# Swapping the first two loads of a decode kernel: a 256 KB load in 2 KB rows ahead of a 4 MB load in 32 KB rows

## The chip, the cores and the metric

The kernel runs on one core of one Trainium2 chip. Times are device microseconds (us) of a whole execution. The profile's "span" runs from the first to the last instruction and is about 1.2 us shorter. Before, three executions took 659.73, 659.74 and 659.96 us. The check of the result counts a difference as faster or slower only at 2%.

Words used below: a *load* is one copy from memory to the core's on-chip buffers; an *issue* is the instruction that starts it; the *queue* is the list of issued loads that the sixteen DMA engines work off; a *packet* is one row of a load as one engine moves it. K0, V0, K1, V1, K2 are the successive 4 MB pieces of the key and value caches. *wq* and *wo* are the weights of the query and output projections. The *prologue* is the compute work before the loop over the pieces. PE multiplies matrices, DVE and ACT work on vectors, POOL makes constants and small copies, and SP does nothing here but issue loads and wait.

## The reference

One decode step, batch 2, one token: attention over a cache of 8192 positions with 32 heads of 128, then a gated feed-forward layer.

```python
q = layernorm(x) @ wq                       # x: 2 x 512, wq: 512 x 4096
p = softmax(q . k_cache * 128 ** -0.5)      # k_cache, v_cache: 2 x 32 x 8192 x 128, bf16
h = x + (p @ v_cache) @ wo                  # wo: 4096 x 512
n = layernorm(h)
out = h + (relu(n @ W_gate) * (n @ W_up)) @ W_down
```

The caches are 2 x 134 MB, and each byte is used once. All weights together are 12.6 MB.

## The kernel before

The caches pass through four slots of 4 MB (32 KB in each of 128 partitions). K pieces use slots 0 and 2, V pieces 1 and 3. All large loads are issued by one engine, SP, whose instructions run in order. wq borrows slot 3 until the query is made; the last 256 rows of wo (`wo_rows`) go to a scratch area, and the remaining 3.8 MB of wo are loaded later.

```python
def load(s, cache, p):
    nc.sync.dma_start(slot[s][:], kv(cache, p)).then_inc(slot_sem[s], 16)

nc.scalar.dma_start(x_row, A_x[:, 0]).then_inc(sem_x, 16)
nc.sync.dma_start(slot[3][:], A_wq.rearrange("(p c) n -> p (c n)", c=DC)).then_inc(sem_wq, 16)   # 128 rows of 32 KB
nc.sync.dma_start(
    wo_rows, A_wo[128 * DR:].rearrange("(p r) n -> p (r n)", r=2)).then_inc(sem_wl, 16)           # 128 rows of 2 KB
load(0, A_k_cache, 0)      # K0
load(1, A_v_cache, 0)      # V0
load(2, A_k_cache, 1)      # K1
# ... constants, layernorm of x, its transpose xlT (done at 5.5 us; its token is t_xlT)
pe.wait((sem_wq, 16), t_xlT, t_zero)
# ... 32 matmuls make the query (t_q is the token of the last)
# ... the query is laid out for DVE and PE (q_all)
sp.wait(t_q)               # wq has been used: slot 3 is free
load(3, A_v_cache, 1)      # V1
nc.sync.dma_start(X[:], A_wo[0:128 * DR] ...)       # the rest of wo, 3.8 MB
# ...
pe.wait((sem_wl, 16))      # wo_rows are used here, after the query layout
# ... two pairs of matmuls put them into wo_last
dve.wait(t_q_b, t_wl, t_const)                      # then the loop starts
# in the loop, for each piece p:
#   DVE multiplies K by the query (k_mult); after it K's slot is free
sp.wait((d2s, p + 1), tokp("kf", p))
load(s, A_k_cache, p + 2)
```

So V1 can be issued only after the projection has read wq out of slot 3, and K2 only after the first product on DVE, which needs the query and both wo and wq. These are the two ways in which the start can hold up the queue.

The softmax here doesn't subtract the row's maximum and nothing guards it: scores larger than these inputs give would overflow.

## Time and profile before

| | before |
|---|---|
| time, median | 659.74 us |
| span | 658.6 us |
| bytes moved, mean rate | 281.17 MB, 427 GB/s |
| busiest compute engine (DVE) | 71% of the span |
| DMA engines busy with the queue of loads | 99.4% |
| first packet of wq starts | 1.83 us |
| first projection matmul (wq landed) | 12.99 us |
| first K product on DVE | 26.79 us |
| K2 issued | 33.43 us |

These are lines of the page of before: the span, the busy time of the engines, the DMA share in forty slices of the span (tenths), the rate in each slice, the totals and the queue of loads.

```profile
span 658.6 us, 7569 instructions
...
PE 326.1 (50%) x3066; PEld 192.1 (29%) x3067; DVE 469.4 (71%) x280; ACT 214.2 (33%) x433; POOL 72.7 (11%) x125
...
DMA  8999999999999999999999999999999999999997
GB/s 366 445 426 437 426 442 418 442 420 444 424 436 438 422 440 420 444 422 438 430 432 438 422 440 420 444 422 438 440 422 436 424 438 424 440 428 436 434 415 307
DMA packets 10645, 281.17 MB, mean 427 GB/s; under 512 B 1190, under 2 KB 1292, under 8 KB 1804
...
q1 hardware_dynamic: 10628, 281.06, 99.4%
```

What to see: the row of nines. No compute engine is near full, but the queue is, from the first slice to the last. Such a kernel's time is the start of the queue, plus its bytes, plus what comes after the last byte.

The next lines are the timeline of before: start in us, duration in us, engine, line, operation, output<-inputs; in brackets the idle time before it and what ended it. "SPq" lines are issues.

```profile
0.81 0.40 SPq L174 DMA_DIRECT2D slot<-in_A_wq_dram  x1
1.27 0.42 SPq L175 DMA_DIRECT2D prod<-in_A_wo_dram  x1
1.73 0.42 SPq L171 DMA_DIRECT2D slot<-in_A_k_cache_dram  x1
...
12.99 3.58 PE L256 MATMUL O<-slot,xlT 128*2 128x512 bf16 x32 [7.64 <-DMA slot<-in_A_wq_dram]
...
16.61 0.33 SPq L171 DMA_DIRECT2D slot<-in_A_v_cache_dram  x1
...
17.46 1.01 PE L268 MATMUL W<-ident,prod 128*128 128x128 bf16 x8 [0.89 <-DVE prod L265]
...
26.79 6.56 DVE L539 TENSOR_TENSOR prod<-slot,q_c 128x12288 bf16<-128x12288 bf16 x1 [5.78 <-ACT wo_last L328]
...
33.43 0.33 SPq L171 DMA_DIRECT2D slot<-in_A_k_cache_dram  x1
```

Compute waits 7.64 us for wq, so wq looks urgent. But the first K product ends at 33.35 us, K2 is issued then, and three loads (K1, whose first packets are under way, V1 and the rest of wo) are still in the queue.

The trace also holds a record of each packet (start, duration, size). Views of the page do not list them, so they are given here as figures. In the steady part a 32 KB packet takes 1.213 us and one engine starts the next 1.2095 us later; 16 x 32768 B / 1.2095 us is 433 GB/s. The sixteen first packets of wq start at 1.83 to 2.64 us and take 1.39 to 2.22 us, so they lose 0.66 us each on average against 1.213 us. This is called the start-up loss below.

### The profile page before, as it was taken

How to read it: one execution, taken by the hardware profiler on the slowest of the kernel's cores; microseconds unless marked ns; L12 is line 12 of the kernel's file. 1: busy time of each engine (PE TensorE's matmuls, PEld its weight loads, DVE VectorE, ACT ScalarE, POOL GpSimd, SP SyncE). 2: the span in 40 equal slices, each digit the busy share in tenths (PEclk: the TensorE clock that was granted, in tenths of full speed). 3: DMA queues.
4: the chain of work that ended last, by engine and by line, in shares of the span. 5: the costliest groups of instructions: out<-in, count | busy, mean ns of one | idle time of the engine just before them, and what ended most of it. 6: DMA issues, size and time to landing. Idle time of an engine off the chain costs nothing.

```text
span 658.6 us, 7569 instructions
## 1 busy us (share of the span) xinstructions
PE 326.1 (50%) x3066; PEld 192.1 (29%) x3067; DVE 469.4 (71%) x280; ACT 214.2 (33%) x433; POOL 72.7 (11%) x125
## 2 busy tenths in 40 slices
PE   2753444435554354644535453554445454454586
PEld 0431322214332132422213232322323222232354
DVE  1585576788767678776768867677876767787991
ACT  1622332243342233334223243323324322433151
POOL 3001002020200202020020201102020010202000
PEclk9999565565576555576655577555566755557567
DMA  8999999999999999999999999999999999999997
GB/s 366 445 426 437 426 442 418 442 420 444 424 436 438 422 440 420 444 422 438 430 432 438 422 440 420 444 422 438 440 422 436 424 438 424 440 428 436 434 415 307
DMA packets 10645, 281.17 MB, mean 427 GB/s; under 512 B 1190, under 2 KB 1292, under 8 KB 1804
## 3 DMA queue, kind: packets, MB, share of 16 engines
q1 hardware_dynamic: 10628, 281.06, 99.4%
q8 instruction: 5, 0.08, 0.0%
q14 instruction: 4, 0.03, 0.0%
q10 hardware_dynamic: 8, 0.00, 0.0%
HBM read 281.05 MB, written 0.00 MB: 427 GB/s over the span
## 4 chain that ended last, share of the span: by engine, by line
DMA 80%; DVE 18%; issue 1%; SPq 0%; DVEq 0%; PE 0%
DMA slot<-in_A_k_cache_dram 76%; DVE prod L539 16%; DMA slot<-in_B_W_down_dram 4%; DVE prod L548 2%; DVE scores L553 0%; SPq L171 0%; SPq L702 0%; SPq L698 0%; DVE kT L815 0%; DVEq L586 0%; PE O L807 0%; DVEq L590 0%; SPq L175 0%; SPq L174 0%; DVE zi L505 0%
## 5 line engine op out<-in xcount | busy, mean ns | idle before, releaser
L539 DVE TENSOR_TENSOR prod<-slot,q_c 128x12288 bf16<-128x12288 bf16 x32 | 209.9, 6558 | 148.1 <-DMA slot<-in_A_k_cache_dram 141.4
L404 PE MATMUL O<-slot,e 128*16 128x512 bf16 x1024 | 117.2, 609 | 219.3 <-ACT e L494 146.3
L548 DVE TENSOR_TENSOR prod<-prod 128x6144 bf16<-128x6144 bf16 (+3 forms) x128 | 212.3, 1658 | 7.8
L565 ACT ACTIVATE kT<-T 128x1024 bf16<-128x1024 bf16 x128 | 126.2, 1022 | 144.6 <-PE T L380 141.7
L380 PE MATMUL T<-ident_f,slot 128*128 128x128 f32 x512 | 112.8, 376 | 29.4 <-DVEq L586 29.4
L404 PEld LDWEIGHTS O<-slot,e 128*16 128x16 bf16 x1024 | 26.1, 112 | 284.6 <-ACT e L494 172.9
L494 ACT ACTIVATE e<-scores 64x96 bf16<-64x96 f32 x64 | 19.5, 304 | 239.8 <-DVEq L600 237.0
L380 PEld LDWEIGHTS T<-ident_f,slot 128*128 128x128 f32 x512 | 81.9, 193 | 44.4 <-DVEq L586 43.6
L536 POOL COPY q_c<-q_all 128x136 bf16<-128x136 bf16 x32 | 56.3, 1760 | 196.4 <-DVEq L590 152.5
L363 PE MATMUL S<-q_c,kT 128*128 128x4 bf16 x1024 | 47.6, 168 | 39.2 <-ACT kT L565 38.5
L363 PEld LDWEIGHTS S<-q_c,kT 128*128 128x128 bf16 x1024 | 39.6, 104 | 66.8 <-ACT kT L565 65.5
L416 PE MATMUL Ob<-sel,os_sb 128*128 128x4 f32 x136 | 31.0, 351 | 24.0 <-ACT os_sb L568 24.0
L416 PEld LDWEIGHTS Ob<-sel,os_sb 128*128 128x128 f32 x136 | 29.5, 319 | 25.9 <-ACT os_sb L568 25.9
L519 POOL MEMSET O_l<- 128x40 bf16 (+1 forms) x13 | 1.8, 136 | 303.9 <-DVEq L597 303.9
L553 DVE TENSOR_REDUCE scores<-prod 128x96 f32<-128x768 bf16 x32 | 30.5, 953 | 2.8
L565 ACT ACT_TABLE_LOAD x15 | 19.2, 1283 | 0.3
L494 ACT ACTIVATE e<-S 64x32 bf16<-64x32 f32 x64 | 13.0, 203 | 15.1 <-PE S L363 14.7
L568 ACT ACTIVATE os_sb<-O 128x512 f32<-128x512 f32 x17 | 10.2, 597 | 11.6 <-PE O L404 11.3
L494 ACT ACTIVATION_READ_ACCUMULATOR e<-S 64x1 f32 x64 | 12.8, 201 | 0.7
L494 ACT ACTIVATION_READ_ACCUMULATOR e<-scores 64x1 f32 x64 | 11.8, 184 | 0.0
L425 PEld LDWEIGHTS Ob<-zs,ones_f 128*128 128x128 f32 x30 | 7.1, 294 | 12.8 <-issue 12.8
L524 POOL COPY rsel<-rows 128x30 bf16<-128x30 bf16 x28 | 5.9, 209 | 33.3 <-DVEq L597 32.5
(104 smaller groups left out, 90.6 us busy)
## 6 DMA issues: line engine op xcount, KB each, us to landing
slot<-in_A_k_cache_dram SPq DMA_DIRECT2D x32, 4096.0 KB, 32.1
slot<-in_A_v_cache_dram SPq DMA_DIRECT2D x31, 4096.0 KB, 30.3
slot<-in_A_wq_dram SPq DMA_DIRECT2D x1, 4096.0 KB, 12.1
X<-in_A_wo_dram SPq DMA_DIRECT2D x1, 3840.0 KB, 46.0
slot<-in_A_v_cache_dram SPq DMA_DIRECT2D x1, 3072.0 KB, 23.1
slot<-in_B_W_up_dram SPq DMA_DIRECT2D x1, 1376.0 KB, 21.7
slot<-in_B_W_gate_dram SPq DMA_DIRECT2D x1, 1376.0 KB, 24.7
slot<-in_A_v_cache_dram SPq DMA_DIRECT2D x1, 1024.0 KB, 25.2
```

Source lines behind the costliest of these rows:

```text
L363: i = nc.tensor.matmul(Sp[p % 2][:, 2 * jj:2 * jj + 4], lhsT=kv_[:, k, r, :], rhs=q_c[p % 2][:, 4 * r:4 * r + 4], start=(r == 0), stop=(r ...
L380: i = nc.tensor.transpose(Tp[g % 2][:, k * 128:(k + 1) * 128], k_t[:, j:j + 2, :].rearrange("p j d -> p (j d)").bitcast(F32), ident_f[:])
L404: i = nc.tensor.matmul(Op[0][c:c + 16, :], lhsT=e_t[q][:, j // VJ, :], rhs=v_t[:, j:j + VJ, :].rearrange("p j d -> p (j d)"), start=(q == ...
L416: i = nc.tensor.matmul(Ob[:, 0:4], lhsT=os_sb[:, jj * Dh:(jj + 1) * Dh], rhs=sel[:, 4 * jj:4 * jj + 4], start=(jj == 0), stop=(jj == VJ - 1))
L425: return nc.tensor.matmul(bank[:, ZC:ZC + 8], lhsT=ones_f[:], rhs=zs[:], start=True, stop=True)
L494: i = nc.scalar.activation(out=e_t[q][h, j0 // VJ:j1 // VJ, 8 * q:8 * q + 8].rearrange("p g (j a) -> p g j a", a=2)[:, :, :, a], in_=src(h ...
L536: nc.gpsimd.tensor_copy(out=q_c[p % 2][:], in_=q_all[:, p]).then_inc(g2d, 1)
L539: return nc.vector.tensor_tensor(out=prod[:, 0:JC, :], in0=tile((2 * p) % 4)[:, 0:JC, :], in1=q_c[p % 2][:, 8:QW].unsqueeze(1).broadcast_t ...
L548: run(nc.vector.tensor_tensor(out=prod[:, 0:JC, 0:w], in0=prod[:, 0:JC, 0:w], in1=prod[:, 0:JC, w:2 * w], op=ALU.add))
L553: return nc.vector.tensor_reduce(out=scores[p % PG][:, 0:JC], in_=prod[:, 0:JC, 0:8], axis=AX.X, op=ALU.add)
L565: to_pe(nc.scalar.activation(out=kT[gg % 2][:], in_=Tp[gg % 2][:].bitcast(BF16), func=ACT.Copy))
L568: to_pe(nc.scalar.activation(out=os_sb[:], in_=Op[0][:], func=ACT.Copy))
```

## The change

The intent is to let the program's first load be a small one in short rows, with the big load in long rows behind it. Two issues swap places; nothing is added, removed or resized.

```diff
                 nc.scalar.dma_start(x_row, A_x[:, 0]).then_inc(sem_x, 16)
-                nc.sync.dma_start(slot[3][:], A_wq.rearrange("(p c) n -> p (c n)", c=DC)).then_inc(sem_wq, 16)
                 nc.sync.dma_start(
                     wo_rows, A_wo[128 * DR:].rearrange("(p r) n -> p (r n)", r=2)).then_inc(sem_wl, 16)
+                nc.sync.dma_start(slot[3][:], A_wq.rearrange("(p c) n -> p (c n)", c=DC)).then_inc(sem_wq, 16)
                 load(0, A_k_cache, 0)
```

## The prediction

> **What bounds the kernel now.** One queue of loads that never runs dry. The page counts 281.17 MB at a mean of 427 GB/s over a span of 658.6 us; the queue holds 99.4% of the DMA engines' time, and the forty slices show nine tenths everywhere but in the first and last. In the trace's packet records a steady 32 KB packet starts 1.2095 us after the one before: 16 x 32768 B / 1.2095 us = 433 GB/s. The Trainium skill ("DMA: Bandwidth & Descriptors", Specifications) states a fabric ceiling of 435 GB/s; the trace agrees to half a per cent. The sixteen engines run free of each other: the spread of 0.36 us between them after their first packet is the same seven packets later. So the end is the slowest engine's start plus a fixed amount of work, plus the FFN tail.
>
> **What the change does.** No byte, row or instruction is added; two issues at the head of the queue swap. Before (timeline, packet records):
> - wq is issued at 0.81, wo's rows at 1.27, K0 at 1.73 us; an issue takes 0.40 to 0.42 us.
> - Each engine gets 8 wq packets of 32 KB. The first starts at 1.83 to 2.64 us and takes 1.39 to 2.22 us instead of 1.213: the start-up loss.
> - Each engine's 8 wo packets of 2 KB follow, 0.080 us apart: 0.64 us.
> - The first projection matmul starts at 12.98 us, when wq has landed.
>
> After, wo goes first and wq's packets come 0.64 us later. wq is issued 0.46 us after wo, so its descriptors should be there before wo's work and the start-up loss are over: no bubble, at most 0.1 to 0.2 us in some engine.
>
> **What of it is on the critical path.**
> - wq lands 0.5 to 0.7 us later; the projection, the first K product (26.79 us) and the issue of K2 (33.43 us) slide with it. That is free: when K2 is issued, K1, V1 and the 3.8 MB of wo are still ahead of it, over 25 us of transfer.
> - wo landing earlier is worth nothing: its matmul at 24.3 us waits for the queries.
> - What remains is the start-up. If the loss on the first packets is a matter of time (cold memory, descriptors still being written), nothing changes. If it grows with the packet's length, or comes from sixteen engines starting on rows 32 KB apart, rows of 2 KB save part of some 0.6 us. If the issue cannot feed 2 KB packets, up to 0.2 us is lost.
>
> **Prediction.** 659.5 us, 8 in 10 between 658.8 and 660.2; a change of about -0.2 us. Faster by over 2%: 0.01; within 2%: 0.98; slower by over 2%: 0.01.
>
> **What would show it right or wrong.** Right: the first projection matmul at 13.4 to 13.8 us; K0's packets starting at 12.9 to 13.2 us as before, or up to 0.6 us sooner; the loop's K issues 38.85 us apart per two pairs as before; DMA at nine tenths in all middle slices. The start-up step is wrong if K0's first packets move by more than 0.7 us either way. "No bubble" is wrong if engines stand idle between the last wo and the first wq packet.
>
> **What would make it wrong.** A different phase between the engines that changes the steady packet time (0.3% would show as 2 us), an instruction fetch that falls on the slowest engine[...], or a slow start of the 2 KB packets.

## The result, and the profile after

| | before | after |
|---|---|---|
| time, median (6 runs each) | 659.81 us | 659.82 us |
| range | 659.66 to 660.02 | 659.59 to 660.08 |
| span of the profiled run | 658.6 us | 658.5 us |
| first projection matmul | 12.99 us | 13.70 us |
| first K product | 26.79 us | 26.78 us |
| K2 issued | 33.43 us | 33.42 us |
| sixteen first K0 packets start at | 12.86 to 13.22, mean 13.079 us | 12.78 to 13.32, mean 13.076 us |

The ratio after over before is 1.000, with a 95% interval of 0.9987 to 1.0013. A ratio here is the mean time of one kernel's fast runs over that of the other's fast runs of the same rounds, so it is not quite the ratio of the medians in the table. The experiments below were run in three batches on three chips (11, 13 and 5); each ratio is to before on the same chip, while the traces of the start are compared across chips. The page of after, the lines that answer to those of before:

```profile
span 658.5 us, 7570 instructions
...
DMA  8999999999999999999999999999999999999997
GB/s 368 443 432 429 428 440 422 442 424 436 432 428 432 430 440 422 440 428 432 434 428 434 428 442 422 438 430 430 434 430 434 426 440 424 436 434 428 430 420 310
DMA packets 10645, 281.17 MB, mean 427 GB/s; under 512 B 1190, under 2 KB 1292, under 8 KB 1804
...
q1 hardware_dynamic: 10628, 281.06, 99.3%
```

Packets, bytes and mean rate are the same. The timeline of after:

```profile
0.81 0.40 SPq L174 DMA_DIRECT2D prod<-in_A_wo_dram  x1
...
1.27 0.42 SPq L176 DMA_DIRECT2D slot<-in_A_wq_dram  x1
...
13.70 3.54 PE L256 MATMUL O<-slot,xlT 128*2 128x512 bf16 x32 [8.36 <-DMA slot<-in_A_wq_dram]
...
17.29 0.33 SPq L171 DMA_DIRECT2D slot<-in_A_v_cache_dram  x1
...
18.14 0.61 PE L268 MATMUL W<-ident,prod 128*128 128x128 bf16 x8 [0.89 <-DVE prod L265]
...
26.78 6.56 DVE L539 TENSOR_TENSOR prod<-slot,q_c 128x12288 bf16<-128x12288 bf16 x1 [5.57 <-ACT wo_last L328]
...
33.42 0.33 SPq L171 DMA_DIRECT2D slot<-in_A_k_cache_dram  x1
```

The wait for wq grew from 7.64 to 8.36 us, the projection slid by 0.71 us, and V1's issue by 0.68 us. The first K product did not slide: the transposes of L268 took 0.61 us in place of 1.01 us, and the matmuls behind them were shorter too. More on this below.

The packet records show the start-up loss in another form. In after the 2 KB packets of wo begin at 1.85 us, but between 2.2 and 2.4 us only 6.5 of the sixteen engines are busy, and between 2.4 and 2.6 us only 9.3. Then the first wq packets start at 2.82 to 3.19 us and take 1.36 to 1.91 us, again longer than 1.213 us. When both loads are through, at K0's first packets, the two kernels stand within 0.003 us of each other.

### The profile page after: what moved, and what is told of

Same layout as the page of the kernel before. It is cut to its first block, busy times and chain, and to the rows that moved or that the text cites. A ratio compares the mean times of both kernels' runs of the same rounds, so it can differ in the third digit from the quotient of the medians.

```text
span 658.5 us, 7570 instructions
## 1 busy us (share of the span) xinstructions
PE 323.8 (49%) x3067; PEld 189.8 (29%) x3067; DVE 469.3 (71%) x280; ACT 214.3 (33%) x433; POOL 73.4 (11%) x125
## 4 chain that ended last, share of the span: by engine, by line
DMA 80%; DVE 15%; PE 3%; ACT 1%; issue 0%; DVEq 0%; SPq 0%
DMA slot<-in_A_k_cache_dram 69%; DVE prod L539 15%; DMA slot<-in_A_v_cache_dram 5%; DMA slot<-in_B_W_gate_dram 4%; DMA slot<-in_A_wq_dram 2%; PE O L404 1%; PE O L256 1%; ACT q_all L317 0%; PE O L311 0%; ACT kT L565 0%; PE T L324 0%; PE O L755 0%; PE O L807 0%; PE Ob L416 0%; PE T L380 0%
## 5 line engine op out<-in xcount | busy, mean ns | idle before, releaser
L404 PE MATMUL O<-slot,e 128*16 128x512 bf16 x1024 | 117.1, 609 | 220.6 <-ACT e L494 146.2
L380 PE MATMUL T<-ident_f,slot 128*128 128x128 f32 x512 | 111.1, 372 | 30.0 <-DVEq L586 29.1
L404 PEld LDWEIGHTS O<-slot,e 128*16 128x16 bf16 x1024 | 26.2, 111 | 285.8 <-ACT e L494 172.9
L380 PEld LDWEIGHTS T<-ident_f,slot 128*128 128x128 f32 x512 | 80.5, 190 | 45.2 <-DVEq L586 43.3
L494 ACT ACTIVATION_READ_ACCUMULATOR e<-S 64x1 f32 x64 | 12.8, 201 | 0.7
L425 PEld LDWEIGHTS Ob<-zs,ones_f 128*128 128x128 f32 x30 | 7.4, 306 | 12.8 <-issue 12.8
```

The lines of the kernel that those rows point to most:

```text
L380: i = nc.tensor.transpose(Tp[g % 2][:, k * 128:(k + 1) * 128], k_t[:, j:j + 2, :].rearrange("p j d -> p (j d)").bitcast(F32), ident_f[:])
L404: i = nc.tensor.matmul(Op[0][c:c + 16, :], lhsT=e_t[q][:, j // VJ, :], rhs=v_t[:, j:j + VJ, :].rearrange("p j d -> p (j d)"), start=(q == ...
L425: return nc.tensor.matmul(bank[:, ZC:ZC + 8], lhsT=ones_f[:], rhs=zs[:], start=True, stop=True)
L494: i = nc.scalar.activation(out=e_t[q][h, j0 // VJ:j1 // VJ, 8 * q:8 * q + 8].rearrange("p g (j a) -> p g j a", a=2)[:, :, :, a], in_=src(h ...
```

## The experiments

Theory: the queue is first in, first out and never dry, so the order of its first loads is free, as long as compute still refills it in time; the start-up loss belongs to the start of the stream and not to the load that happens to be first. Rivals: (a) there was a gain at the head that was given back later; (b) each microsecond that the prologue slips costs something, and 0.7 us was too little to see; (c) the loss depends on the first load's rows, or (d) on the five issues that are made one after another just then.

The measure of the start, besides the time, is the mean start of the sixteen packets that follow wq and wo (K0's first packets), from the packet records.

### before_again: the kernel before, a second trace

No edit.

> The kernel before, unchanged, for a second trace of its start. All theories: time 659.6 to 660.1 us. It says how far the start itself scatters: the sixteen first K0 packets started at 12.858 to 13.222 us (mean 13.079) in the first trace; I expect the mean within 0.15 us of that, the first wq packets again 1.4 to 2.2 us long, and the first projection matmul within 0.15 us of 12.99.

Measured: 659.65 us (one run, its state therefore unknown). The first wq packets took 1.64 to 2.30 us, K0's packets started at a mean of 13.089 us (before: 13.079), and the projection began at 13.06 us. This is as expected, but for longest first packets a little over the 2.2 us named. What was not expected: the first K product came 2.5 us earlier than in the first trace of the same kernel. Its timeline:

```profile
13.06 3.21 PE L256 MATMUL O<-slot,xlT 128*2 128x512 bf16 x32 [7.73 <-DMA slot<-in_A_wq_dram]
...
24.33 6.56 DVE L539 TENSOR_TENSOR prod<-slot,q_c 128x12288 bf16<-128x12288 bf16 x1 [4.08 <-ACT wo_last L328]
...
50.96 0.33 SPq L171 DMA_DIRECT2D slot<-in_A_k_cache_dram  x1
```

From projection to K product this run took 11.27 us, the first trace 13.80 us. The issue of K3 (last line) is at 50.96 us against 50.94 us in the first trace: a prologue that is 2.5 us faster has left no mark by then.

### hold_wq_first and hold_wo_first: only two loads in the queue at the start

```diff
-                load(0, A_k_cache, 0)
-                load(1, A_v_cache, 0)
-                load(2, A_k_cache, 1)
 ...
+                sp.wait(t_xlT)             # x has been transposed: 5.5 us
+                load(0, A_k_cache, 0)
+                load(1, A_v_cache, 0)
+                load(2, A_k_cache, 1)
```

The first has the order of before, the second the order of after.

> Order of before (wq, wo), but K0, V0 and K1 are issued only when x has been transposed (about 5.5 us), not at 1.7 to 3.2 us. Issue theory (the start-up loss is the descriptors of five loads being made while the first packets run): first wq packets shrink from 1.39-2.22 to about 1.25-1.5 us, K0's packets start at a mean of about 12.5 us, and the loss shows up again as long packets between 5.5 and 8 us or the time falls by about 0.5 us. Time theory (the first 2 us of traffic are slow whatever is issued) and length theory (the first 32 KB packet of an engine is slow): first packets as before, K0's mean start at 13.0-13.2 us, time within 0.3 us of before.

> Order of after (wo, wq), with K0, V0 and K1 held until about 5.5 us. Issue theory: the wq packets behind wo shrink from 1.36-1.91 to about 1.22-1.4 us, K0's mean start falls from 13.08 to about 12.5 us. Time and length theories: as in after, 13.0-13.2 us. If the order of the two head loads matters at all once the other issues are out of the way, it shows as a difference to hold_wq_first of over 0.2 us in K0's start; my theory of a conserved queue says under 0.1 us.

| | K0's mean start | first wq packets | time | ratio to before (95%) |
|---|---|---|---|---|
| before | 13.079 us | 1.39 to 2.22 us | 659.79 us | |
| hold_wq_first | 13.010 us | 1.34 to 2.22 us | 659.85 us | 1.0002 (0.9988 to 1.0015) |
| after | 13.076 us | 1.36 to 1.91 us | 659.82 us | |
| hold_wo_first | 12.945 us | 1.21 to 2.03 us | 659.68 us | 0.9998 (0.9984 to 1.0012) |

The loss in hold_wq_first is 0.61 us against 0.66 us. Rival (d), which asked for K0 at about 12.5 us, falls: at most about 0.1 us of the loss can be due to the three other issues. (After 5.6 us some packets are then 1.238 to 1.246 us long in place of 1.213 us, so even that small part may only have moved.) The difference between the two orders is 0.065 us, below the 0.2 us that would have counted.

### wo_fifth: the small load behind 12 MB of cache

```diff
-                nc.sync.dma_start(
-                    wo_rows, A_wo[128 * DR:].rearrange("(p r) n -> p (r n)", r=2)).then_inc(sem_wl, 16)
                 load(0, A_k_cache, 0)
                 load(1, A_v_cache, 0)
                 load(2, A_k_cache, 1)
+                nc.sync.dma_start(
+                    wo_rows, A_wo[128 * DR:].rearrange("(p r) n -> p (r n)", r=2)).then_inc(sem_wl, 16)
```

> Order wq, K0, V0, K1, wo: the small load goes behind 12 MB of cache. My theory (a never-empty first-in first-out queue: order within it is free as long as compute is not needed to refill it): K0's packets start 0.65 us earlier (mean about 12.43), wo lands at about 42 us, the first K product starts at about 45 us in place of 26.8, K2 is issued at about 52 us, still ahead of the end of the queue at about 62 us, and the time is 659.8 +- 0.3 us. Rival (a slip of the prologue delays the end, and in the change it was just too small to see): about 18 us more, 678 us.

Measured: 660.0 us, ratio 1.0004 (0.9988 to 1.0019). K0's packets start at a mean of 12.419 us, 0.66 us earlier, which is wo's work: moved, not saved. Its timeline shows the slip:

```profile
13.17 3.22 PE L256 MATMUL O<-slot,xlT 128*2 128x512 bf16 x32 [7.83 <-DMA slot<-in_A_wq_dram]
...
45.85 6.56 DVE L539 TENSOR_TENSOR prod<-slot,q_c 128x12288 bf16<-128x12288 bf16 x1 [25.48 <-ACT wo_last L328]
...
52.50 0.33 SPq L171 DMA_DIRECT2D slot<-in_A_k_cache_dram  x1
```

DVE is idle for 25.48 us and the first K product is 19.1 us late, and the time does not move. Rival (b) asked for 678 us.

### wq_fourth and wq_fifth: how far may wq slip?

Both start from after. wq goes behind V0 (order wo, K0, V0, wq, K1), or behind K1 (order wo, K0, V0, K1, wq):

```diff
-                nc.sync.dma_start(slot[3][:], A_wq.rearrange("(p c) n -> p (c n)", c=DC)).then_inc(sem_wq, 16)
                 load(0, A_k_cache, 0)
                 load(1, A_v_cache, 0)
                 load(2, A_k_cache, 1)
+                nc.sync.dma_start(slot[3][:], A_wq.rearrange("(p c) n -> p (c n)", c=DC)).then_inc(sem_wq, 16)
```

(This is wq_fifth; in wq_fourth the line stands one load higher.)

> Order wo, K0, V0, wq, K1: wq comes 19.4 us later than in after. My theory: first projection matmul at about 33 us, first K product at 44 to 46 us, K2 issued at 51 to 53 us while the queue lasts until about 61 us; time 659.8 +- 0.3 us. Rival (each microsecond that the projection slips costs something): at least 1 us more.

> Order wo, K0, V0, K1, wq: wq comes 29.1 us later than in after and is now the last thing in the queue, and V1 is only issued after the projection. My theory: the projection starts at about 42.7 us, the queue is dry from about 42.4 us until V1's first packets at about 47.5 us, and the time is 4.8 to 5.8 us more (664.6 to 665.6 us), all of it this one hole, which the windows show as a DMA share near zero between 43 and 47 us. If the time stays at 659.8 us, my account of what makes an order free is wrong.

| | first projection matmul | V1 issued | first K product | K2 issued | time | ratio to before (95%) |
|---|---|---|---|---|---|---|
| after | 13.70 | 17.29 | 26.78 | 33.42 | 659.82 us | |
| wq_fourth | 33.11 | 36.73 | 44.74 | 51.38 | 659.70 us | 0.9999 (0.9982 to 1.0016) |
| wq_fifth | 42.75 | 46.38 | 56.48 | 63.13 | 666.39 us | 1.0097 (1.008 to 1.0114) |

A slip of 19.4 us is free, one of 29 us is not. The windows of wq_fifth show why; columns are the stretch and its length, busy time and instructions of PE, PE's weight loads, DVE, ACT and POOL, the granted clock of PE (it also reads 1.00 where no clock is recorded yet, here up to 55.32 us), the DMA share and the rate (a packet is counted where it starts):

```profile
41.00:42.00 1.00, 0.00 (x0) 0.00 (x0) 0.00 (x0) 0.00 (x0) 0.00 (x0) 1.00 0.16 66
42.00:47.00 5.00, 3.58 (x32) 0.90 (x32) 0.61 (x1) 0.60 (x1) 0.00 (x0) 1.00 0.00 0
47.00:49.00 2.00, 1.46 (x14) 1.07 (x16) 0.53 (x4) 0.00 (x0) 0.00 (x0) 1.00 0.95 262
49.00:60.00 11.00, 8.54 (x52) 3.62 (x49) 5.11 (x9) 8.85 (x14) 0.55 (x2) 0.94 0.99 429
```

The queue is dry while the projection runs, because V1 could not be issued before it had read wq out of slot 3. The size was missed: I expected 4.8 to 5.8 us more, it was 6.55 us (666.39 less 659.84). By the packet records, V1's first packets come 5.36 us later than in before, and its packets pay the start-up loss again (1.43 to 2.18 us long), so that K2's first packets come 5.99 us later. A second thin place follows at 76.6 to 77.8 us, where as few as 11.5 of sixteen engines are busy: V2 was issued at 75.31 us, just before K2's last packets. After it the delay is 6.7 us on average over the engines and stays there (packets of the steady loop near 500 us are 6.7 us late too). My sum had the first hole alone. These figures are of the profiled run, the slowest of the four (667.38 us; the four range from 665.79 to 667.38). In it the engines are less in step than in before: the loop's issues are 7.5 us late (261.89 against 254.36 us), and the time is 7.54 us over before's. So the two holes account for most of the cost; that the slowest engine's lag behind that mean makes up the rest is likely, but not shown.

### wq_rows_8k: the first load in shorter rows

```diff
-nc.sync.dma_start(slot[3][:], A_wq.rearrange("(p c) n -> p (c n)", c=DC)).then_inc(sem_wq, 16)
+nc.sync.dma_start(slot[3][:].rearrange("p (c n) -> p c n", c=DC),
+                  A_wq.rearrange("(c p) n -> p c n", c=DC)).then_inc(sem_wq, 16)
 ...
-    rv = row.rearrange("b (n c) -> b c n", c=DC)
+    rv = row.rearrange("b (n c) -> b c n" if k == 0 else "b (c n) -> b c n", c=DC)
```

> Order of before, but wq in rows of 8 KB (four times as many packets; the normalised x is split the same way, so the result is right). Holding the other issues left the start-up loss standing, so two theories are left. Length theory (the first packet of an engine is slow because it is 32 KB long): the loss of 0.66 us shrinks, K0's packets start at a mean of 12.5-12.8 us. Time theory (the first two microseconds of a stream are slow, whatever its rows): K0's mean start is 13.08 us plus some 0.1 us for the extra packets, about 13.2 us. Time of the kernel in both cases within 0.5 us of before.

Measured: K0's mean start is 13.333 us, the time 660.11 us, ratio 1.0005 (0.9988 to 1.0021). In the steady part an 8 KB packet starts 0.306 us after the one before it, so 32 of them take 9.79 us where 8 packets of 32 KB take 9.68 us. That explains 0.11 us of the 0.25 us by which K0 is later than in before; the expected 13.2 us allowed for no more than that. The start-up loss has not shrunk; it is spread over several packets: the first sixteen took 0.35 to 1.08 us, later ones 0.309 us. Rival (c) in this form, that a long first row causes the loss, falls.

### all_held: the whole queue starts later

```diff
-                nc.sync.dma_start(slot[3][:], A_wq ...)        # and wo_rows, K0, V0, K1
 ...
+                sp.wait(t_xlT)
+                nc.sync.dma_start(slot[3][:], A_wq ...)        # and wo_rows, K0, V0, K1, in the order of before
```

> Order of before, but all five loads of the synchronising engine are held until x has been transposed (5.57 us in place of 0.81 us). My theory (the queue is the whole time, so its start moves the end one for one): 4.76 us more, 664.5 us, between 664.1 and 664.9. Rival (there is slack in the compute or the tail that takes a late start up): under 2 us more. For the start-up loss: if it belongs to the first microseconds of the program, the wq packets now start at full rate (1.21-1.30 us) and K0's mean start is about 17.2 us; if it belongs to the first moments of any stream of loads, they are 1.4-2.2 us again and K0's mean start is about 17.8 us.

Measured: 664.72 us, ratio 1.0075 (1.0059 to 1.0092), which is 4.88 us more than before's 659.84 us in the same rounds. The first issue moved by 4.76 us:

```profile
5.57 0.40 SPq L241 DMA_DIRECT2D slot<-in_A_wq_dram  x1
...
17.93 3.40 PE L257 MATMUL O<-slot,xlT 128*2 128x512 bf16 x32 [12.59 <-DMA slot<-in_A_wq_dram]
```

So the start of the queue moves the end one for one, within the scatter. And the start-up loss went with it: the first wq packets start at 6.59 us and lose 0.69 us each on average (1.29 to 2.43 us long), and K0's mean start is 17.835 us, 4.756 us after before's 13.079. It is not the first microseconds of the program that are slow, but the first of a stream that starts from rest. V1's packets in wq_fifth, after the hole, say the same at 47.3 us. What causes it stays open; no run here looks inside it.

### after_again: the kernel after, a second trace and five more rounds

No edit.

> The kernel after, unchanged, for a second trace of its start and five more rounds against before. My theory: the same time, ratio 0.999 to 1.001, K0's packets starting at a mean of 12.9 to 13.1 us as before's two traces did (13.08, 13.09). The first projection matmul again 0.5 to 0.8 us after before's 12.99 and 13.06 us, while the first K product may stand anywhere from 24.8 to 27.6 us, since it moved by 2.5 us between two traces of before. Rival (a true gain at the head that the first rounds could not resolve): K0's mean start below 12.8 us in this trace too and a ratio of 0.999 or less.

Measured: 659.70 us against 659.94 us of before in the same rounds, ratio 0.9999 (0.9985 to 1.0012). K0's mean start is 12.910 us, the projection starts at 13.72 us, the first K product at 26.84 us. The two traces of after differ by 0.17 us in K0's start, those of before by 0.01 us. On average after's head is 0.09 us ahead ((13.079 + 13.089 - 13.076 - 12.910) / 2). Two traces each do not make that a gain, and if it were one, it would be 0.014% of the time. Rival (a) asked for K0 below 12.8 us and is not supported. Note that this trace's first packets of wo start only at 2.14 us (after: 1.85 us), and K0 is still no later: what agrees between the traces is the time from the first issue to K0, not the start or length of the first packets alone. A gain or loss of under about 0.8 us, the half width of the interval, cannot be excluded by the times alone.

## Why the prediction was right or wrong

The time of 659.5 us, range 658.8 to 660.2, held: 659.82 us. The class "within 2%" held. The time alone says little about the start-up step, since the range would have held with the saving and without it; the experiments decide that. Point by point:

1. **The queue is the time.** Right, and shown. Moving its start by 4.76 us moved the end by 4.88 us (all_held); a hole of 5 us in it, with what follows from it, cost 6.55 us (wq_fifth); 19 us of waiting on the compute side cost nothing (wo_fifth, wq_fourth). The Trainium skill ("DMA: Bandwidth & Descriptors", Queues, rings and completion order) says that each engine consumes descriptors in ring order. The packet records agree: in after each engine's first wq packet starts at most 0.006 us after the start of the 4-byte write that ends its share of wo (the semaphore write). The loop's K issues in after stay 38.85 us apart per two pairs (390.49 and 429.34 us), as predicted.

2. **"wq lands 0.5 to 0.7 us later."** Right: 0.71 us at the projection, 0.68 us at V1's issue.

3. **"The projection, the first K product and the issue of K2 slide with it."** Wrong for the last two. They stood at 26.78 and 33.42 us, as before. The stretch from projection to K product was 13.80 us in before and 13.08 us in after, and 11.27 us in before's second trace. It scatters by more than the slip. In the traces the difference is matmul speed: the first two query-layout matmuls of L311 took 614 ns in before and 383 ns in after. These are the lines of before:

```profile
18.92 1.04 PE L311 MATMUL O<-prod 128*64 128x512 bf16 x4
...
20.23 1.12 PE L311 MATMUL O<-prod 128*64 128x512 bf16 x4 [0.27 <-ACT q_all L317]
```

And of after, where the last line counts twelve matmuls:

```profile
19.15 0.60 PE L311 MATMUL O<-prod 128*64 128x512 bf16 x4
...
20.23 3.78 PE L311 MATMUL O<-prod 128*64 128x512 bf16 x12 [0.48 <-ACT q_all L317]
```

The Trainium skill ("TensorE: Matmul & The Clock Gate", Part 1) describes an array clock that doubles after some 3.4 us of activity, in windows that run free of the kernel, so that the same kernel can meet it at different points. The clock records in the traces show both speeds, in stretches of 3.41 us or multiples of it. In after the full clock is recorded from 17.07 us, 3.37 us after the first projection matmul, to 20.49 us, and half the clock from then on; the L311 matmuls that start before 20.49 us took 379 to 423 ns, the later ones 632 to 637 ns. In before_again it is recorded from 15.76 to 29.42 us, and all sixteen took 379 to 403 ns. In before there is no record until 62.27 us, though PE was busy for 8.12 of the 10 us from 14 to 24 us, and all sixteen took 614 to 637 ns, so the rule of 3.4 us alone does not say when the clock rises; the profile's clock column reads 1.00 there only because nothing is recorded. So it is luck that the first K product stands at 26.78 us beside 26.79: a faster clock made good the slip of 0.71 us, and the swap is not needed for it, since before_again had it longer in the old order. What sets the moment at which the clock rises, no run tested. That the slip would be free, which carried the prediction, was right for a better reason than its size: up to 19 us are free.

4. **"No bubble."** Right where it was placed: no engine waits between the last wo and the first wq packet. But engines do stand idle inside the wo load (6.5 of sixteen busy at 2.2 to 2.4 us). That is the start-up loss in another form, not an added one: K0 starts at the same time, within the scatter.

5. **The start-up loss, left open between "nothing changes" and "rows of 2 KB save part of some 0.6 us".** The first was right. The loss did not shrink with 8 KB rows, shrank by at most about 0.1 us when the other issues were held, and came back whole when the stream was started 4.76 us later. Swapping the two loads only changes which packets pay it.

6. **The size, "about -0.2 us".** Measured +0.01 us between the medians, -0.003 us at K0's start in the first pair of traces and -0.18 us in the second. The term that was mis-sized is the saving on the first packets; the runs show none that can be told from the scatter.

## What to carry to other kernels

Where one first-in, first-out queue of loads is full from start to end, the order of the loads at its head is worth nothing; what counts is when the first one is issued and whether the queue ever runs dry. To see how much a load may be moved back, ask which later issue depends on it and how much is still queued when that issue is made: here 19 us of slip were free and 29 us cost 6.5 us. A long wait of a compute engine for a load (7.6 us for wq, even 25 us for wo) is no reason to hurry that load, if the wait does not reach the queue.

## What the Trainium skill lacked or had wrong

- "DMA: Bandwidth & Descriptors" has a first-byte delay and a fixed cost of a load, but no slow start of a stream's first packets. Here the first 32 KB of each engine took 1.3 to 2.4 us in place of 1.213 us in three streams that began from rest, at 1.83 us (before), 6.59 us (all_held) and 47.3 us (wq_fifth). With a load in 32 KB rows first it cost 0.6 to 0.7 us on average over the engines, on top of the first byte's delay.
- The same page (Bandwidth, "Where 436 GB/s comes from") says without a condition that loads from memory are bound at about 358 GB/s per core; only the note under the table before it limits that figure to both cores of a pair streaming. Here one core loaded at 433 GB/s in the steady part and 427 GB/s over the whole span; its fabric ceiling of 435 GB/s is the figure that fits.
- The same page's first-byte delay of about 0.6 us for such issues (Latency and other measured facts) agrees: from the end of the first issue to the first packet it was 0.62 us in before (1.21 to 1.83 us) and in all_held (5.97 to 6.59 us). But it was 0.93 us in after_again (1.21 to 2.14 us), so it is not always met.
- "TensorE: Matmul & The Clock Gate" (Part 1) warns that clock events in a trace have been seen to be unreliable. In the traces here they agree with the matmuls: in before the 128x512 matmuls of L404 took 379 ns in the median where the full clock is recorded and 634 ns where half of it is. What can mislead is the 1.00 that the clock column shows before the first record (point 3).
